# Softmax and values by halves in three attention units of a two-layer decode step

## The chip, the core and the metric

The kernel runs on one core of a Trainium2 chip. The core has five engines with an instruction stream each: TensorE (PE in the profile; its weight loads are shown apart as PEld), VectorE (DVE), ScalarE (ACT), GpSimd (POOL) and SyncE (SP), which here only issues transfers. Work on different engines is ordered by semaphores alone. The metric is the device time of one execution in microseconds (us); lower is better.

## The reference

Two equal layers are applied to four tokens (batch B = 4, model width 512), each a cached attention and then a gated unit, both behind a layer norm:

```python
q = (layernorm(x) @ wq)                       # 32 heads of 128
k = repeat(k_cache, 4); v = repeat(v_cache, 4)  # 8 heads of 4096 x 128 in the cache
p = softmax(q @ k.T * 128 ** -0.5)
x = x + (p @ v) @ wo
g, u = layernorm(x) @ w_gate, layernorm(x) @ w_up   # width 1792
x = x + (sigmoid(g) * u) @ w_down
# ... and the same again with the same weights and caches
```

All inputs are bf16. The caches are 33.6 MB each for K and for V, and both layers read them.

## The kernel before, in words

**Units.** The attention is cut into 16 units. A unit is one token `b`, one half `hg` of the cache heads (four of eight) and one layer `l`. Their order is written out in the list `seq`. Units 5, 9, 13 and 15 are (0,0,1), (1,0,1), (2,0,1) and (3,0,1): the last unit of a token, in layer two, with heads 0 to 3. Units 6, 10 and 14 are the units (b,1,1) of the next token.

**Tiles and the ring.** K and V come in tiles of 128 x 2048 bf16 (512 KB): one cache head, and one half `q` of the positions. So a unit has eight K tiles (q = 0: four heads, q = 1: four heads) and eight V tiles. They share a ring of 23 slots in the on-chip memory. The K tiles and seven of the V tiles of a unit (b,1,0) are kept in their slots until unit (b,1,1) has used them, so that layer two loads just one tile for that unit. While they are kept, eight slots are left for all the others. That is so when units 5, 9 and 13 stream their sixteen tiles, and right after each of them a unit with kept tiles follows.

**A unit before.** `unit_scores` transposes each K tile in place on VectorE (L656, a 32 x 32 block transpose) and then, for each q, issues 16 score matmuls into half of the bank pair `S_ps` (L663) as one block. `unit_probs` takes one maximum over all 1024 columns (L677) and spreads it over the heads by a transpose, a minimum and a transpose (L678, L680, L686). ScalarE writes the exponentials with their sums (L689). Eight matmuls into `PT_ps` (L696), a copy (L701), sixteen matmuls (L707) and a copy (L715) turn them into `pt_sb`. A sum over partitions (L721) and a reciprocal (L725) give the weight `wcol`. `unit_values` multiplies by V: 16 matmuls for q = 0 and 16 for q = 1, both accumulated in `O_ps` (L739). It scales the result into `o_sb` (L745), transposes it (L750), copies it to `oT` (L760) and multiplies by `wo` in 64 small matmuls (L766); L781 adds it to the token's state. When both head halves of a token are done, `chain` runs the gated unit (`layer_norm` L793 to L808, `rstd` L817 to L826, `glu` L842 to L894) and, after layer one, the queries of layer two (`second_q`, L614 and L620; `spread`, L634 and L641, which writes the score operand `qbd`).

**What sets the order.** Nothing is ordered by hand. Every step is put into a plan (`_Plan.put`) with an engine, a cost in us, a rank (the unit's number; half a unit more for its chain) and what it reads and writes. `schedule` then runs a list schedule when the kernel is built: each engine takes the step that can start first, the lower rank first among equals, and may wait a little for a lower rank (`PATIENCE`). The order of the transfers on SP's queue is fixed: in unit i, V of unit i - 1 and then K of unit i. A transfer into the ring waits for all users of the tile that held its slot; which slot that is, the plan decides by its own times. PE's time in the plan (`_Tensor`) has two speeds, as the clock gate has, and a wait at each block of instructions that has to be fetched (`PAGE`, `FETCH`). Where the plan sees PE idle, it puts in filler matmuls into an unused bank (`F_ps`, L936), which keep the clock up. `emit` writes each engine's stream in the planned order, with waits on semaphores, so a plan that is wrong in its times is still carried out in its order.

**Locks.** The PSUM bank `M_ps` is shared by many short steps. A step with `lock="M"` takes it and one with `free="M"` gives it back. `G_ps` and `U_ps` are used by the gated unit and by `second_q`.

## Time and profile before

| | |
|---|---|
| median of three runs | 332.08 us (331.55 to 333.64) |
| profiled execution, its own time | 331.62 us |
| span of its instructions | 329.7 us |
| mean granted TensorE clock | 0.948 |
| DVE busy | 177.5 us (54%) |
| ACT busy | 64.6 us (20%) |
| PE busy, fillers included | 291.7 us (88%); L936, the fillers, 137.3 us of it |
| DMA | 117.34 MB, mean 356 GB/s |

A line of the profile gives an engine, a kernel line, an operation, what it writes and reads, and its shape (partitions x elements). In the groups, "busy" is the time of all of them, then follow the mean duration in ns and the idle time of the engine before them. In a timeline, the first number is the start and the second the duration of a merged run, both in us, and the end of the line in brackets is the idle time before it and what ended it. "SPq" is SP's queue, which issues transfers; a transfer's issue is not its landing. In a table of stretches each row has a stretch's bounds, its length, the busy time and the number of instructions of each engine, the granted clock, the busy share of the DMA engines and their rate.

### The profile page before, as it was taken

Reading aid. Unit: us, or ns where it says so; the run is one execution under the profiler, and the core shown is the slowest. Engines: PE = TensorE matmul, PEld = TensorE weight load, DVE = VectorE, ACT = ScalarE, POOL = GpSimd, SP = SyncE. Lnnn points to the kernel's source line nnn. Section 1 sums busy time; section 2 is a strip of 40 time slices with the busy share of each in tenths; the row PEclk is TensorE's granted clock in tenths of the full one; section 3 lists DMA queues with packets and bytes.
Section 4 is the critical chain, followed back from the end, with each engine's and each line's share of the span. In section 5 each row is a group of like instructions: output and inputs, shape, how many; then the busy total and the mean of one; then the engine's idle time right before and its main releaser. Section 6 shows DMA issues by size and latency. Waiting matters only on the chain.

```text
span 329.7 us, 10495 instructions
## 1 busy us (share of the span) xinstructions
PE 291.7 (88%) x4772; PEld 143.2 (43%) x4772; DVE 177.5 (54%) x325; ACT 64.6 (20%) x137; POOL 12.3 (4%) x36
## 2 busy tenths in 40 slices
PE   6998999989979878989888689998869999998986
PEld 2534434434454433453454244543444444644433
DVE  5771482009613863942874828735827649329602
ACT  1202102002021312121223032121332121313221
POOL 5100000000000000000000000000000000000000
PEclk9997999999997999987997999969997999879999
DMA  7999999999999999698999999888999998979910
GB/s 278 380 410 408 410 371 356 408 411 406 381 357 366 416 408 408 238 352 285 393 412 409 408 407 397 291 325 329 416 407 410 407 409 268 361 263 412 408 59 0
DMA packets 35408, 117.34 MB, mean 356 GB/s; under 512 B 3364, under 2 KB 7716, under 8 KB 35364
## 3 DMA queue, kind: packets, MB, share of 16 engines
q1 hardware_dynamic: 35312, 116.67, 92.9%
q8 instruction: 37, 0.61, 0.7%
q14 instruction: 7, 0.06, 0.0%
q10 hardware_dynamic: 52, 0.01, 0.0%
HBM read 116.66 MB, written 0.00 MB: 354 GB/s over the span
## 4 chain that ended last, share of the span: by engine, by line
DMA 33%; PE 27%; SPq 17%; issue 13%; DVE 6%; ACT 3%; POOL 1%; ACTq 0%; POOLq 0%; DVEq 0%
DMA ring<-in_A_k_cache_dram 19%; SPq L486 13%; DMA wo<-in_A_wo_dram 6%; PE S_ps L663 5%; PE F_ps L936 5%; PE O_ps L739 4%; DMA wd_r<-in_B_w_down_dram 4%; SPq L489 4%; DMA ring<-in_A_v_cache_dram 4%; DVE ring L656 3%; PE U_ps L614 3%; PE U_ps L886 2%; ACT p_sb L689 1%; PE M_ps L766 1%; PE G_ps L842 1%
## 5 line engine op out<-in xcount | busy, mean ns | idle before, releaser
L656 DVE STREAM_TRANSPOSE ring<-ring 128x1024 int32<-128x1024 int32 x96 | 116.4, 1232 | 51.2 <-DMA ring<-in_A_k_cache_dram 50.4
L936 PE MATMUL F_ps<-ident 128*128 128x512 bf16 x524 | 137.3, 392 | 3.3 <-POOL stat L437 3.3
L936 PEld LDWEIGHTS F_ps<-ident 128*128 128x128 bf16 x524 | 47.8, 102 | 62.4 <-issue 17.4
L663 PE MATMUL S_ps<-ring,qbd 128*16 128x512 bf16 x512 | 39.8, 433 | 4.9 <-DVE ring L656 4.7
L739 PE MATMUL O_ps<-ring,pt_sb 128*16 128x512 bf16 x512 | 36.8, 418 | 7.0 <-DMA ring<-in_A_v_cache_dram 4.0
L677 DVE TENSOR_REDUCE ml<-S_ps 128x1 f32<-128x1024 f32 x16 | 19.6, 1224 | 34.0 <-PE S_ps L663 34.0
L689 ACT ACTIVATE p_sb<-S_ps,tr 128x1024 bf16<-128x1024 f32 x16 | 17.8, 1113 | 54.7 <-DVE tr L686 53.9
L745 ACT ACTIVATE o_sb<-O_ps,stat 128x512 bf16<-128x512 f32 x16 | 11.0, 687 | 77.8 <-PE O_ps L739 77.8
L739 PEld LDWEIGHTS O_ps<-ring,pt_sb 128*16 128x16 bf16 x512 | 12.4, 94 | 28.7 <-issue 15.2
L663 PEld LDWEIGHTS S_ps<-ring,qbd 128*16 128x16 bf16 x512 | 12.1, 94 | 23.8 <-DVE ring L656 9.8
L766 PE MATMUL M_ps<-wo,oT 128*1 128x128 bf16 x1024 | 17.2, 219 | 2.5 <-issue 1.7
L614 PE MATMUL U_ps<-xT,wq 128*128 128x1 bf16 x512 | 15.6, 164 | 3.9 <-issue 3.7
L826 POOL TENSOR_TENSOR stat<-stat 128x1 f32<-128x1 f32 x12 | 6.5, 540 | 302.9 <-DVE stat L822 264.4
L614 PEld LDWEIGHTS U_ps<-xT,wq 128*128 128x128 bf16 x512 | 14.8, 97 | 6.6 <-issue 5.1
L766 PEld LDWEIGHTS M_ps<-wo,oT 128*1 128x1 bf16 x1024 | 14.2, 83 | 6.8 <-ACT oT L760 3.8
L725 DVE RECIPROCAL stat<-M_ps 128x1 f32<-128x1 f32 x16 | 2.7, 166 | 20.9 <-PE M_ps L721 20.9
L859 ACT ACTIVATE p_sb<-G_ps,stat 128x256 f32<-128x256 f32 x8 | 3.8, 475 | 46.1 <-POOL stat L826 33.4
L701 ACT ACTIVATE p_sb<-PT_ps 128x512 bf16<-128x512 f32 x16 | 9.5, 597 | 12.3 <-PE PT_ps L696 12.3
L715 ACT ACTIVATE pt_sb<-PT_ps 128x512 bf16<-128x512 f32 x16 | 9.6, 598 | 11.7 <-PE PT_ps L707 11.7
L842 PE MATMUL G_ps<-wg,xT 128*1 128x448 bf16 x128 | 9.0, 351 | 2.6 <-DVE xT L799 2.1
L707 PE MATMUL PT_ps<-p_sb,ident 128*32 128x128 bf16 x256 | 7.7, 244 | 3.3 <-ACT p_sb L701 1.9
L641 DVE TENSOR_TENSOR qbd<-M_ps,stat 128x256 bf16<-128x256 f32 x16 | 6.5, 404 | 7.6 <-PE M_ps L634 7.6
(92 smaller groups left out, 177.5 us busy)
## 6 DMA issues: line engine op xcount, KB each, us to landing
ring<-in_A_v_cache_dram SPq DMA_DIRECT2D x100, 512.0 KB, 13.8
ring<-in_A_k_cache_dram SPq DMA_DIRECT2D x96, 512.0 KB, 12.8
wq<-in_A_wq_dram SPq DMA_DIRECT2D x2, 2048.0 KB, 14.3
wo<-in_A_wo_dram SPq DMA_DIRECT2D x4, 1024.0 KB, 14.7
wg<-in_B_w_gate_dram SPq DMA_DIRECT2D x1, 1792.0 KB, 13.5
wu<-in_B_w_up_dram SPq DMA_DIRECT2D x1, 1792.0 KB, 18.2
wd<-in_B_w_down_dram SPq DMA_DIRECT2D x1, 1536.0 KB, 22.6
wd_r<-in_B_w_down_dram SPq DMA_DIRECT2D x2, 128.0 KB, 18.4
```

Of the source, the lines that this page charges most:

```text
L486: S.put("sp", lambda e: e.dma_start(ring[t.slot], src), dma="ring", load=t, size=0.524, cost=0.45)
L489: S.put("sp", lambda e: e.dma_start(o, i), writes=[key], dma=key, size=size * pace, cost=0.45)
L614: fns.append(lambda e, g=g, k=k, c0=c0, c=c: e.matmul(U_ps[:, 16 + c:17 + c], lhsT=wq[:, g // NS, k, c0:c0 + DH], rhs=xT[:, b, k:k + 1], s ...
L656: "dve", lambda e, t=t: e.transpose(ring[t.slot].bitcast(dt.int32), ring[t.slot].bitcast(dt.int32)),
L663: fns.append(lambda e, s=s, t=t, nn=nn, q=q: e.matmul(S_ps[32 * s:32 * s + 16, q * 512:(q + 1) * 512], lhsT=qbd[:, qi, nn, s, :], rhs=ring ...
L677: dve(lambda e: e.tensor_reduce(ml[:, 0:1], S_ps[:], AX.X, ALU.max, negate=True), ["S0", "S1"], ["ml"], 1.22)
L689: lambda e: e.activation(p_sb[:].rearrange("p c x -> p (c x)"), S_ps[:], ACTF.Exp, bias=tr[:, 0:1], accum_out=ls),
L739: fns.append(lambda e, s=s, v=v, c=c, cc=cc: e.matmul(O_ps[32 * s:32 * s + 16, :], lhsT=pt[:, c, s, :, :].rearrange("p t h -> p (t h)"), r ...
L745: "act", lambda e: e.activation(o_sb[:], O_ps[:], ACTF.Copy, scale=wcol[:, i % 2:i % 2 + 1]),
L766: fns.append(lambda e, n=n, j=j: e.matmul(M_ps[32 * j:32 * j + 1, P:2 * P], lhsT=oT[:, i % 2, n:n + 1], rhs=wo[:, hg * 16 + n, j * P:(j + ...
L842: fns.append(lambda e, k=k, j=j: e.matmul(o_ps[32 * j:32 * j + 1, 0:FS], lhsT=xT[:, b, k:k + 1], rhs=w[:, k, j * FS:(j + 1) * FS], start=( ...
L936: lambda e: e.matmul(F_ps[:], lhsT=ident[:], rhs=ident[:].unsqueeze(1).broadcast_to([P, 4, P]), start=True, stop=True,),
```

## The change

In units 5, 9 and 13 the softmax and the product with V are done separately for q = 0 and q = 1. Each half has its own maximum, exponentials, sums and transposed weights (`half_probs`), right behind its scores. Each half of V goes into its own bank, q = 0 into `O_ps` and q = 1 into `G_ps` (`half_values`). `half_weights` works out two weights from the two maxima and sums, by which the two results are scaled when they are copied to `o_sb`; their transposes are added up in columns 32 to 47 of `U_ps`. In the same units the scores are issued for two K tiles at a time (eight matmuls) and not for four.

The plan changes as well. A fetched block of instructions counts 126.2 matmuls instead of 128, the count starts at 25.5, and the fp32 matmuls, which are two instructions in the trace, count twice (`wide`). Every step that gives back the bank M gets rank -1, so it goes ahead of all others that could start at the same time.

The diff, cut to its core:

```diff
@@ -18,7 +18,8 @@
 WINDOW = 3.413
 BUSY_UP = 0.8
 BUSY_DOWN = 0.6
-PAGE = 128
+PAGE = 126.2
+PAGE_AT = 25.5
 FETCH = 5.8
 PE_GAP = 0.1
 FILL_FROM = 0.0
@@ -34,7 +35,7 @@
         self.fast = False
         self.window = 0.0
         self.busy = 0.0
-        self.count = 0
+        self.count = PAGE_AT
         self.page = {0: 0.0, 1: 0.0}
 
...
         todo = n
-        while todo:
-            p, at = divmod(self.count, PAGE)
+        while todo > 1e-3:
+            p = int((self.count + 1e-3) / PAGE)
             t = max(t, self.page[p])
             if p + 1 not in self.page:
                 self.page[p + 1] = t + FETCH
-            k = min(PAGE - at, todo)
+            k = min(PAGE * (p + 1) - self.count, todo)
             t = self._part(t, quick * k / n, slow * k / n)
             self.count += k
             todo -= k
...
+        self.words = len(fns)
...
-    def put(self, eng, fns, reads=(), writes=(), cost=0.1, rank=0.0, dma=None, size=0, lock=None, free=None, tiles=(), load=None, cold=None):
+    def put(self, eng, fns, reads=(), writes=(), cost=0.1, rank=0.0, dma=None, size=0, lock=None, free=None, tiles=(), load=None, cold=None, wide=False):
         if not isinstance(fns, (list, tuple)):
             fns = [fns]
         op = _Op(len(self.ops), eng, list(fns), cost, rank, dma or eng, 16 if dma else 1)
         op.size, op.lock, op.free, op.tile = size, lock, free, load
+        op.words *= 2 if wide else 1
+        if free is not None:
+            op.rank = -1.0
...
-            clock[e] = tensor.run(at, op.cost, op.cold, len(op.fns)) if e == "pe" else at + op.cost
+            clock[e] = tensor.run(at, op.cost, op.cold, op.words) if e == "pe" else at + op.cost
...
+    ls2 = stat[:, 41:43]
+    nbh = stat[:, 43:45]
+    nbm = stat[:, 45:46]
+    e2 = stat[:, 46:48]
+    j2 = stat[:, 48:50]
+    wh = stat[:, 56:58]
+    lt = stat[:, 58:59]
+    HALF = (5, 9, 13)
...
-    def unit_scores(i):
+    def half_scores(i, q, parts):
         b, hg, l = seq[i]
         qi, rank = i % 2, float(i)
-        for q in range(2):
-            ts = [tile("k", b, hg, l, s, q) for s in range(NS)]
-            for s, t in enumerate(ts):
+        for part in parts:
+            ts = [(s, tile("k", b, hg, l, s, q)) for s in part]
+            for s, t in ts:
                 if fresh("k", hg, l, s, q):
                     S.put(
                         "dve", lambda e, t=t: e.transpose(ring[t.slot].bitcast(dt.int32), ring[t.slot].bitcast(dt.int32)),
@@ -659,17 +672,149 @@
                     t.users.append(S.ops[-1])
             fns = []
             for nn in range(NQ):
-                for s, t in enumerate(ts):
+                for s, t in ts:
                     fns.append(lambda e, s=s, t=t, nn=nn, q=q: e.matmul(
                         S_ps[32 * s:32 * s + 16, q * 512:(q + 1) * 512],
                         lhsT=qbd[:, qi, nn, s, :],
                         rhs=ring[t.slot].rearrange("p (t bb j r) -> p t bb j r", bb=2, j=32, r=2)[:, :, nn // 2, :, nn % 2],
                         start=(nn == 0), stop=(nn == NQ - 1),
                     ))
-            S.put("pe", fns, reads=[f"qbd{qi}"], writes=[f"S{q}"], tiles=ts, cost=0.86, rank=rank)
+            S.put("pe", fns, reads=[f"qbd{qi}"], writes=[f"S{q}"], tiles=[t for s, t in ts], cost=0.86, rank=rank)
+
+    def half_probs(i, q):
+        rank = float(i)
+        s_ps = S_ps[:, q * 512:(q + 1) * 512]
+        pk = ("p_sb", "p_hi")[q]
+
+        def dve(fn, reads, writes, cost):
+            S.put("dve", fn, reads=reads, writes=writes, cost=cost, rank=rank)
+
+        dve(lambda e: e.tensor_reduce(ml[:, 0:1], s_ps, AX.X, ALU.max, negate=True), [f"S{q}"], ["ml"], 0.68)
+        dve(lambda e: e.transpose(tr[:], ml[:]), ["ml"], ["tr"], 0.22)
+        dve(
+            lambda e: e.tensor_reduce(
+                ml[:].rearrange("p (x h) -> p x h", h=R),
+                tr[:, 0:16].rearrange("p (a h) -> p h a", h=R).unsqueeze(1).broadcast_to([P, 8, R, 4]), AX.X, ALU.min,
+            ),
+            ["tr"], ["ml"], 0.4,
+        )
+        dve(lambda e: e.transpose(tr[:], ml[:]), ["ml"], ["tr"], 0.22)
+        S.put(
+            "act",
+            lambda e: e.activation(
+                p_sb[:, 4 * q:4 * q + 4, :].rearrange("p c x -> p (c x)"), s_ps, ACTF.Exp, bias=tr[:, 0:1],
+                accum_out=ls2[:, q:q + 1],
+            ),
+            reads=[f"S{q}", "tr"], writes=[pk, f"ls2{q}"], cost=0.82, rank=rank,
+        )
+        S.put(
+            "act", lambda e: e.activation(nbh[:, q:q + 1], tr[:, 0:1], ACTF.Copy),
+            reads=["tr"], writes=[f"nbh{q}"], cost=0.2, rank=rank,
+        )
...
+        S.put("pe", fns, reads=[pk, "ident"], writes=["PT"], cost=0.11, rank=rank)
+        S.put(
+            "act",
+            lambda e: e.activation(
+                p_sb[:, 4 * q:4 * q + 2, :].rearrange("p u x -> p (u x)"), PT_ps[:, q * 256:(q + 1) * 256], ACTF.Copy
+            ),
+            reads=["PT"], writes=[pk], cost=0.4, rank=rank,
+        )
...
+        S.put("pe", fns, reads=[pk, "ident"], writes=["PT"], cost=0.16, rank=rank)
+        pt = pt_sb[i % 2]
+        S.put(
+            "act",
+            lambda e: e.activation(
+                pt[:, 4 * q:4 * q + 4].rearrange("p c s t h -> p t (c s) h"),
+                PT_ps[:, q * 256:(q + 1) * 256].rearrange("p (t x h) -> p t x h", t=4, h=R), ACTF.Copy,
+            ),
+            reads=["PT"], writes=[f"pt_sb{i % 2}" + ("", "x")[q]], cost=0.4, rank=rank,
+        )
+
+    def half_weights(i):
+        rank = float(i)
+        S.put(
+            "pe", lambda e: e.matmul(M_ps[:, 20:22], lhsT=hsum[:], rhs=ls2, start=True, stop=True),
+            reads=["ls20", "ls21", "hsum"], writes=[bank("M", True)], cost=0.2, rank=rank, lock="M",
+        )
+        S.put(
+            "dve", lambda e: e.tensor_tensor(nbm, nbh[:, 0:1], nbh[:, 1:2], ALU.min),
+            reads=["nbh0", "nbh1"], writes=["nbm"], cost=0.16, rank=rank,
+        )
+        S.put(
+            "act", lambda e: e.activation(e2, nbh, ACTF.Exp, bias=nbm, scale=-1.0),
+            reads=["nbh0", "nbh1", "nbm"], writes=["e2"], cost=0.22, rank=rank,
+        )
+        S.put(
+            "dve",
+            lambda e: e.scalar_tensor_tensor(
+                out=j2, in0=M_ps[:, 20:22], scalar=1.0, in1=e2, op0=ALU.mult, op1=ALU.mult, accum_out=lt
+            ),
+            reads=[bank("M"), "e2"], writes=["lt", "j2"], cost=0.24, rank=rank, free="M",
+        )
+        S.put("dve", lambda e: e.reciprocal(lt, lt), reads=["lt"], writes=["lt"], cost=0.17, rank=rank)
+        S.put(
+            "dve", lambda e: e.tensor_scalar(wh, e2, lt, None, op0=ALU.mult),
+            reads=["e2", "lt"], writes=["wh"], cost=0.17, rank=rank,
+        )
+
+    def half_values(i, q, parts):
+        b, hg, l = seq[i]
+        rank = float(i)
+        pt = pt_sb[i % 2]
+        o_ps = (O_ps, G_ps)[q]
+        for part in parts:
+            ts = [(s, tile("v", b, hg, l, s, q)) for s in part]
+            fns = []
...
+            S.put(
+                "pe", fns, reads=[f"pt_sb{i % 2}" + ("", "x")[q]], writes=[("O", "G")[q]],
+                tiles=[t for s, t in ts], cost=0.86, rank=rank,
+            )
+        S.put(
+            "act", lambda e: e.activation(o_sb[:], o_ps[:], ACTF.Copy, scale=wh[:, q:q + 1]),
+            reads=[("O", "G")[q], "wh"], writes=["o_sb"], cost=0.7, rank=rank,
+        )
+        S.put(
+            "pe", [
+                lambda e, t4=t4: e.matmul(
+                    U_ps[:, 32:48], lhsT=o_sb[:, t4 * P:(t4 + 1) * P], rhs=id_b[:, :, 4 * t4:4 * t4 + R],
+                    start=(q == 0 and t4 == 0), stop=(q == 1 and t4 == 3),
+                ) for t4 in range(4)
+            ],
+            reads=["o_sb", "ident"], writes=["U"], cost=0.11, cold=0.11, rank=rank,
+        )
+
+    def unit_scores(i):
+        parts = [(0, 1), (2, 3)] if i in HALF else [(0, 1, 2, 3)]
+        for q in range(2):
+            half_scores(i, q, parts)
+            if i in HALF:
+                half_probs(i, q)
 
     def unit_probs(i):
...
+        if i in HALF:
+            half_weights(i)
+            return
...
-            reads=["ls", "hsum"], writes=[bank("M", True)], cost=0.2, rank=rank, lock="M",
+            reads=["ls", "hsum"], writes=[bank("M", True)], cost=0.2, rank=rank, lock="M", wide=True,
...
-    def unit_values(i):
+    def whole_values(i):
...
+    def unit_values(i):
+        b, hg, l = seq[i]
+        rank = float(i)
+        if i in HALF:
+            for q in range(2):
+                half_values(i, q, [(0, 1, 2, 3)])
+        else:
+            whole_values(i)
         o = oT[:, i % 2, :]
         S.put(
             "act",
-            lambda e: e.activation(o, M_ps[:, 0:16], ACTF.Copy),
-            reads=[bank("M")], writes=[f"oT{i % 2}"], cost=0.22, rank=rank, free="M",
+            lambda e: e.activation(o, U_ps[:, 32:48] if i in HALF else M_ps[:, 0:16], ACTF.Copy),
+            reads=["U" if i in HALF else bank("M")], writes=[f"oT{i % 2}"], cost=0.22, rank=rank,
+            free=None if i in HALF else "M",
         )
...
-            reads=[f"xsum{b}", f"x{b}", f"xs{c}", "ones", "sel4"], writes=["U"], cost=0.36, cold=0.8, rank=rank,
+            reads=[f"xsum{b}", f"x{b}", f"xs{c}", "ones", "sel4"], writes=["U"], cost=0.36, cold=0.8, rank=rank, wide=True,
...
-            reads=[f"xsqc{b}", "onesA"], writes=[bank("M", True)], cost=0.2, rank=rank, lock="M",
+            reads=[f"xsqc{b}", "onesA"], writes=[bank("M", True)], cost=0.2, rank=rank, lock="M", wide=True,
...
```

22 lines of the change are left out of this document (21 added, 1 removed).

## The prediction, made before the changed kernel was run

> **What bounds the kernel now.** I read the stretches first: busy time and DMA rate by stretch of time.
>
> ```profile
> 113.00:134.00 21.00, 16.93 (x296) 7.54 (x288) 13.20 (x20) 4.14 (x8) 0.00 (x0) 1.00 1.03 410
> 134.00:146.00 12.00, 10.79 (x228) 6.27 (x228) 8.68 (x22) 2.17 (x5) 0.73 (x2) 0.97 0.76 256
> 146.00:160.00 14.00, 12.92 (x209) 5.96 (x206) 5.37 (x11) 2.23 (x5) 0.35 (x1) 0.78 0.93 329
> 160.00:205.00 45.00, 38.51 (x713) 18.98 (x717) 29.74 (x49) 10.83 (x22) 1.00 (x2) 0.96 1.03 407
> 205.00:217.00 12.00, 11.33 (x226) 6.51 (x218) 8.41 (x20) 2.89 (x7) 0.62 (x2) 0.86 0.89 303
> 217.00:231.00 14.00, 12.02 (x213) 5.53 (x205) 6.88 (x17) 1.62 (x4) 0.22 (x1) 0.88 0.88 328
> 274.00:286.00 12.00, 11.45 (x268) 7.41 (x264) 8.29 (x20) 3.13 (x8) 1.08 (x2) 0.97 0.86 281
> 286.00:298.00 12.00, 10.95 (x192) 4.74 (x192) 3.54 (x8) 1.65 (x4) 0.00 (x0) 0.75 0.82 308
> ```
>
> The last column is GB/s. Outside three stretches the stream of K and V runs at 405 to 410, and no engine can make it faster; I call 409 full. Inside them it starves: 12 x (1 - 256/409) = 4.5 us and 14 x (1 - 329/409) = 2.7 in the first, 3.1 and 2.8 in the second, 3.8 and 3.0 in the third. That is 11.4 in the three front parts, 8.5 in the rear parts, 19.9 in all. They lie at units 5, 9 and 13, where only eight slots are free.
>
> Next come the waits of SP's queue and the timelines of the first stretch, to see what is late:
>
> ```profile
> SPq L311 <- PE S_ps L663: 56.5, 11, 10.1
> SPq L486 <- PE O_ps L739: 23.6, 8, 6.1
> ...
> 126.66 0.33 SPq L486 DMA_DIRECT2D ring<-in_A_k_cache_dram  x1
> 137.13 13.60 SPq L486 DMA_DIRECT2D ring<-in_A_v_cache_dram  x9
> 150.77 4.88 SPq L486 DMA_DIRECT2D ring<-in_A_k_cache_dram  x8
> ...
> 130.00 2.53 DVE L656 STREAM_TRANSPOSE ring<-ring 128x1024 int32<-128x1024 int32 x2
> 135.96 1.08 PE L663 MATMUL S_ps<-ring,qbd 128*16 128x512 bf16 x16
> 148.47 1.88 PE L663 MATMUL S_ps<-ring,qbd 128*16 128x512 bf16 x16
> 150.14 1.92 PE L739 MATMUL O_ps<-ring,pt_sb 128*16 128x512 bf16 x16
> ```
>
> **Front part.** The last K tile is issued at 126.66; then SP waits for the scores of q = 0 (135.96 to 137.04) and issues the first V tile at 137.13. The landing events of the trace put that K tile at 137.5 and that V tile at 141.5: a queue that has run dry needs 4.4 us from issue to landing, and a tile takes 1.27 in a full stream. But the second K tile of the unit was transposed by 131.3. Only the block of four tiles, and the gated unit's matmuls ahead of it on PE, kept two slots until 137. **Rear part.** The first four V tiles have landed by 146.7, and the next slot is free at 150.4, after scores of the kept unit 6 at 148.47; values of unit 5 come at 150.14, because `pt_sb` needs the maximum over both halves (L677 at 140.98, the last copy of L715 at 148.65). In the third stretch the same values run at 287.26 and the next issue is at 289.19. The second is like these.
>
> **The change, part by part.**
>
> *Pairs.* The same matmuls, 2 x 8 for 16; the first pair can run at 131.3 + 8 x 0.07 (1.08 us for 16). V's first two issues move from 137.1 to about 132, before the queue is dry; 137.5 - 4.4 = 133.1 was needed. Front gain: 4.5, 3.1, 3.8, less what the last pair of q = 1 leaves. By the rows that pair needs the last transpose (139.7), the half's extra DVE work (next) and its own 0.6, so 142.4; its V tiles, seventh and eighth behind K at 1.27 each, land at 146.4 without a hole and should be issued at 142.0. I leave 0.5 per stretch; at worst PE is again held by L842 and L886 (1 to 2 us), which is all of the gain.
>
> *Half maxima.* Per unit a second L678, L680, L686 (0.21 + 0.37 + 0.21) and two reductions over 512 columns for one over 1024 (1.224). No row has that shape; each lies between 0.61 (half) and 1.22 (all of it). I take 0.66, near the half: L865 falls from 0.42 to 0.35 between 256 and 192 columns, almost in step with them. `half_weights` adds three steps like L725 and L808 (0.17 each). DVE: 0.79 + 0.10 + 0.5 = 1.4 us per unit, at most 2.5. The first half's four steps with their gaps, some 1.9, fall between the q = 1 transposes, and there DVE has no room: from 128.7 to 139.7 it works almost without a break and ends 0.9 behind the last landing. So the last transpose ends some 2 us later, which is counted above.
>
> *Half exponentials and copies on ACT.* L689 (1.11 + 0.19) becomes twice 0.65 to 1.3; L701 and L715 (0.60) twice 0.35 to 0.6 (L859 with 256 columns: 0.475); L745 (0.69) doubles. Some 2 to 3 us more per unit; ACT is busy 2.2 of the 14 us at 146 to 160 and 3.1 of the 12 at 274 to 286, so this costs nothing unless a half step stands ahead of the gated unit's tanh (a rival below).
>
> *Half values.* q = 0's chain runs while q = 1's K tiles land; its V tiles land by 142.6, values run 142.7 to 143.8, and four slots are free at 143.9, not 150.4. V of q = 1 lands until 147.7, so the next tile, issued at 143.9 + 4.4 = 148.3, costs 0.6. Further slots are due at 149 (values of q = 1, or unit 6's scores at 148.5). Rear gain 2.7, 2.8, 3.0, less 0.7 each. Worst: zero, if these slots wait for the kept unit all the same.
>
> *What is late next.* After the first stretch SP again waits for slots: the last V tile of unit 7 is issued at 167.94, after a hole of 7 us in SP's timeline, and lands 9.0 us later, 4.6 more than a dry queue needs. With the stream 6 us ahead, and unit 6 only some 4 to 5 ahead (its exponential waits for `p_hi`, behind unit 5's gated unit), I give back 0.8, and 0.8 after the second.
>
> After the third the end is not the stream's:
>
> ```profile
> 297.02 1.25 DVE L656 STREAM_TRANSPOSE ring<-ring 128x1024 int32<-128x1024 int32 x1 [1.01 <-DMA ring<-in_A_k_cache_dram]
> 305.25 3.48 DVE L656 STREAM_TRANSPOSE ring<-ring 128x1024 int32<-128x1024 int32 x3
> 310.07 1.22 DVE L677 TENSOR_REDUCE ml<-S_ps 128x1 f32<-128x1024 f32 x1 [1.35 <-PE S_ps L663]
> 317.58 1.04 PE L739 MATMUL O_ps<-ring,pt_sb 128*16 128x512 bf16 x16 [0.62 <-DMA ring<-in_A_v_cache_dram]
> ```
>
> Unit 15 stays whole. DVE works without a break from 297.0 to 308.7 (eight transposes, 10 us, and 1.7 of others), and the way from there to `pt_sb` takes until 315.87; the last V tile lands at 317.54. If K comes 5.5 us earlier, unit 14's maximum (2.3 us, now 293.7 to 296.0, just ahead) and later steps of unit 13 (0.9) fall into this run: 291.5 + 11.7 + 3.2 = 306.4, only 2.3 to 2.7 earlier. `pt_sb` at 313.2, then 32 matmuls in 2.1: values end at 315.3 and not at 318.62. So the third stretch gives 3.3, not its 6.8 - 1.2.
>
> *Plan constants.* `PAGE`, `wide` and rank -1 add no instruction; they shuffle the order. The trace shows what blocks cost: pieces of 1.2 to 2.3 us of "issue" inside PE groups in the chain. Planning them better gains up to 2 us, a worse order loses as much (patience for rank -1 idles DVE at most a third of a transpose). I take 0.4 lost. The Trainium skill's page Runtime: NRT & Kernel Launch (section Instruction fetch mechanics) holds that crossing a block is mostly hidden; by it this term is 0, and these pieces speak against it.
>
> **Sum.** 7.2 - 1.2 - 0.8 = 5.2; 5.9 - 1.2 - 0.8 = 3.9; 3.3; less 0.4: 12.0. From the span, 329.7 - 12.0 = 317.7; the profiled execution has 1.9 outside the span, 319.6, and the median of the runs lies 0.5 above it: **320 us**.
>
> **Rivals.**
> 1. *Only the pairs work.* V slots of q = 0 come no earlier than unit 6's scores; the half chains land in PE's and ACT's queues too late. For it: before, the rear slots came from scores of the kept unit in two of three stretches. Against: 287.26 in the third. Front 11.4 - 1.5, third stretch capped at 3.3, 0.4 lost: 4.0 + 2.6 + 3.3 - 0.4 = 9.5, near 323.
> 2. *All of it and nothing given back.* Each stretch loses 1 us and the end follows the stream: 19.9 - 3 = 17 to 18, near 314. Against: DVE's run at the end.
> 3. *The order undoes it: no change.* The plan's pair costs 0.86 as the four did (a measured pair is about half), so PE's plan is off by up to 1.7 us per unit; a pair placed behind L842, L886 or L614 frees nothing early. Holes move, 328 to 335.
> 4. *Slower: the other token's chain pays.* ACT and DVE run in order. If the first half's maximum (1.9 us) and ACT steps (1.8) stand ahead of the chain of unit 4, 8 or 12 (L799 to L894, then L614), `qbd` of the kept unit comes 3.7 us later, and so do its eight slots: scores at 152, not 148.5. With the rear gain lost and 3.7 x 3 = 11 more starvation against a front gain halved to 5.7: 5.4 slower, near 337. It decides from the point where the kept unit's first scores start over 12 us after the last K landing (now 10.9, 9.1, 11.7). Against: chain ranks (4.5, 8.5, 12.5) go before the half's (5, 9, 13) whenever both can start.
>
> **How the numbers follow.** Forecast 0.45, rival 1 0.22, rival 2 0.12, rival 3 0.10, rival 4 0.11. A measurement of this kernel tells about 1% (3.3 us) from no change. Faster by more: the first three and a little of rival 3, 0.80; within: 0.09; slower by more: 0.11. Range: below, rival 2 with the plan's 2 us and a little, 311; above, rival 3 nearly whole, 334. That leaves out rival 4 and the edges, about 0.15.
>
> **What would show it.** Right: at 134 to 160 and its two fellows 380 GB/s or more; V's first issue of units 5, 9, 13 at least 4 us before the last K landing; L739's q = 0 block right behind the fourth V landing; DVE without a break in the last K tiles, and `pt_sb` of unit 15 after its last V landing. Wrong: a first pair behind L842 on PE; the kept unit's scores later than now; stream rates below 400 between the stretches.

## The result, and the profile after

The changed kernel takes **327.54 us** (median of four runs, 326.84 to 337.07) against 331.99 before: a ratio of 0.987, 95% interval 0.982 to 0.992. An execution over 1.5% slower than the fastest of its kernel, like the one at 337.07, counts in the medians below but not in the ratios, and where such a one was profiled a table has a dash. The forecast was 320. The direction came, and 4.5 of the 12 us.

The profiled execution took 326.88 us, with a span of 324.9 and a granted clock of 0.937. First its stretches of time: bounds, length, busy time of PE, PEld, DVE, ACT and POOL, granted clock, DMA share, GB/s.

```profile
134.00:146.00 12.00, 11.60 (x230) 6.49 (x230) 9.97 (x26) 2.50 (x8) 0.54 (x1) 0.86 0.99 351
146.00:160.00 14.00, 12.75 (x291) 6.68 (x283) 7.01 (x25) 3.53 (x10) 0.54 (x1) 0.88 1.01 363
...
205.00:217.00 12.00, 9.96 (x224) 5.75 (x222) 6.95 (x23) 4.49 (x14) 0.54 (x1) 1.00 0.95 321
217.00:231.00 14.00, 12.82 (x212) 5.69 (x213) 7.42 (x19) 2.93 (x7) 0.54 (x1) 0.88 1.02 387
274.00:286.00 12.00, 10.79 (x270) 7.29 (x270) 6.31 (x16) 2.59 (x11) 0.54 (x1) 0.78 0.79 269
286.00:298.00 12.00, 11.76 (x203) 5.31 (x202) 7.82 (x21) 3.28 (x8) 0.54 (x1) 0.80 1.00 368
```

The stream still starves at units 5, 9 and 13, though less; these windows are fixed in time while the work in them comes up to 8 us earlier than before. So I also counted the holes from the landing events: each landing's distance from the one before, less the size of the tile at full rate, summed over the three stretches. "Next" are the nine tiles that follow V of unit 5, 9 or 13.

| us lost in the stream | V, q = 0 | V, q = 1 | next | all |
|---|---|---|---|---|
| before | 10.0 | 2.3 | 8.6 | 20.9 |
| after | 0.7 | 7.4 | 5.0 | 13.1 |

The hole ahead of V is closed. Another has opened four tiles later, at V of q = 1, and the rear hole is a good half of what it was. From the last landing of V of units 4, 8 and 12 to the next such mark or the end, the stages were 70.2, 69.1 and 60.9 us and are now 66.2, 67.7 and 60.3. The first mark itself moved from 127.4 to 128.6. So the gains are 4.0, 1.4 and 0.6, less 1.2. These are figures of one execution each: the changed kernel profiled once more (after_again below) lost 1.7, 6.1 and 7.2 us, with stages of 67.3, 68.6 and 60.3, so a single one holds to some 2 us.

The timeline of the first stretch, after (start, duration, line, operation; in brackets the idle time before it and what ended it):

```profile
132.53 1.03 PE L676 MATMUL S_ps<-ring,qbd 128*16 128x512 bf16 x8 [2.31 <-DVE ring L669]
133.65 13.03 SPq L499 DMA_DIRECT2D ring<-in_A_v_cache_dram  x9
139.59 0.93 PE L997 MATMUL U_ps<-wu,xT 128*1 128x448 bf16 x16
140.35 1.03 PE L676 MATMUL S_ps<-ring,qbd 128*16 128x512 bf16 x8
143.72 1.07 PE L676 MATMUL S_ps<-ring,qbd 128*16 128x512 bf16 x8 [0.17 <-DVE ring L669]
144.88 1.79 SPq L499 DMA_DIRECT2D ring<-in_A_v_cache_dram  x3
145.26 1.04 PE L784 MATMUL O_ps<-ring,pt_sb 128*16 128x512 bf16 x16
150.72 1.73 PE L784 MATMUL G_ps<-ring,pt_sb 128*16 128x512 bf16 x16 [1.12 <-DMA ring<-in_A_v_cache_dram]
152.58 1.88 PE L676 MATMUL S_ps<-ring,qbd 128*16 128x512 bf16 x16
```

V's first issue comes at 133.65, 5.2 us ahead of the last K landing (138.85). But the first pair of q = 1, transposed by 137.65, runs at 140.35, behind the gated unit's L997. The last pair waits for the last transpose, which ends 4.8 us after the last landing (2.2 before); the third V tile of q = 1 is issued only at 144.88. That is 6.0 us after the last K landing, where the forecast had 4.9 (142.4 after 137.5) and 4.5 was needed. Then the kept unit 6 finds its scores at 152.58 behind the values of q = 1, which wait for V. Its first scores start 13.7, 14.2 and 14.1 us after the last K landing of units 5, 9 and 13 (before: 10.9, 9.0, 11.7).

In the third stretch both pairs are late, and for the first of them it is DVE that is late:

```profile
269.25 1.24 DVE L669 STREAM_TRANSPOSE ring<-ring 128x1024 int32<-128x1024 int32 x1
271.10 0.69 DVE L692 TENSOR_REDUCE ml<-S_ps 128x1 f32<-128x512 f32 x1
273.89 2.36 DVE L669 STREAM_TRANSPOSE ring<-ring 128x1024 int32<-128x1024 int32 x2
275.64 1.03 PE L676 MATMUL S_ps<-ring,qbd 128*16 128x512 bf16 x8
276.42 1.24 DVE L669 STREAM_TRANSPOSE ring<-ring 128x1024 int32<-128x1024 int32 x1
277.07 3.71 SPq L499 DMA_DIRECT2D ring<-in_A_v_cache_dram  x5
278.27 1.04 PE L784 MATMUL O_ps<-ring,pt_sb 128*16 128x512 bf16 x16 [1.06 <-DMA ring<-in_A_v_cache_dram]
279.24 0.55 PE L627 MATMUL U_ps<-xT,wq 128*128 128x1 bf16 x16
279.88 1.37 PE L627 MATMUL U_ps<-xT,wq 128*128 128x1 bf16 x48
281.18 1.88 PE L676 MATMUL S_ps<-ring,qbd 128*16 128x512 bf16 x8
```

The fifth K tile is transposed by 270.49 and the sixth only from 273.89 on: between them DVE does the first half's maximum (L692 and what follows it) and steps of the gated unit. So the first pair of q = 1 runs at 275.64, and the first V tile of q = 1 is issued at 277.07, 4.3 us after the last K landing (272.7). That is 2.2 of the 3.6 us that V of q = 1 loses here. The last pair's tiles are ready at 277.66 (end of the last L669 row). It starts at 281.18, behind the values of q = 0 (L784), which wait for their fourth V tile, and behind the layer-two queries of the gated unit (L627), and it runs slowly (1.88). Its slots come free for tiles behind V; the last two V tiles go into slots of the values of q = 0.

The end, which answers to the rows of unit 15 before:

```profile
298.14 2.36 DVE L669 STREAM_TRANSPOSE ring<-ring 128x1024 int32<-128x1024 int32 x2
301.32 3.48 DVE L669 STREAM_TRANSPOSE ring<-ring 128x1024 int32<-128x1024 int32 x3
306.14 1.23 DVE L822 TENSOR_REDUCE ml<-S_ps 128x1 f32<-128x1024 f32 x1 [1.35 <-PE S_ps L676]
312.00 1.90 PE L884 MATMUL O_ps<-ring,pt_sb 128*16 128x512 bf16 x32
```

The last V tile lands at 310.2 and no longer matters: the values wait for `pt_sb` (L860). Unit 15's transposes end at 304.8, 4.8 us after its last K landing (2.8 before), for DVE does unit 14's maximum and the gated unit of unit 13 among them.

Last, the groups of the score matmuls, from the pages of before and of after (busy time, mean ns of one, idle before). The number of matmuls is the same.

```profile
L663 PE MATMUL S_ps<-ring,qbd 128*16 128x512 bf16 x512 | 39.8, 433 | 4.9 <-DVE ring L656 4.7
```

```profile
L676 PE MATMUL S_ps<-ring,qbd 128*16 128x512 bf16 x512 | 47.3, 439 | 6.0 <-DVE ring L669 5.9
```

7.5 us more for the same 512 matmuls. A pair of eight takes 1.03 to 1.11 us in ten of twelve cases (median 1.07), and a block of sixteen 1.11 (median of 26): both as long. By these medians, twelve pairs in place of six blocks make some 6.2 of the 7.5.

### The profile page after: what moved, and what is told of

Its sections match the earlier page's. It is cut to its first block, busy times and chain, and to the rows that moved or that the text cites. A ratio compares the mean times of both kernels' runs of the same rounds, so it can differ in the third digit from the quotient of the medians.

```text
span 324.9 us, 10574 instructions
## 1 busy us (share of the span) xinstructions
PE 288.7 (89%) x4784; PEld 141.9 (44%) x4784; DVE 182.2 (56%) x349; ACT 69.7 (21%) x161; POOL 12.3 (4%) x36
## 5 line engine op out<-in xcount | busy, mean ns | idle before, releaser
L669 DVE STREAM_TRANSPOSE ring<-ring 128x1024 int32<-128x1024 int32 x96 | 115.7, 1228 | 45.4 <-DMA ring<-in_A_k_cache_dram 44.7
L1091 PE MATMUL F_ps<-ident 128*128 128x512 bf16 x476 | 124.6, 393 | 3.3 <-POOL stat L450 3.3
L1091 PEld LDWEIGHTS F_ps<-ident 128*128 128x128 bf16 x476 | 44.5, 103 | 57.2 <-issue 15.7
L676 PE MATMUL S_ps<-ring,qbd 128*16 128x512 bf16 x512 | 47.3, 439 | 6.0 <-DVE ring L669 5.9
L884 PE MATMUL O_ps<-ring,pt_sb 128*16 128x512 bf16 x416 | 28.8, 414 | 2.7 <-DMA ring<-in_A_v_cache_dram 1.3
L822 DVE TENSOR_REDUCE ml<-S_ps 128x1 f32<-128x1024 f32 x13 | 15.9, 1222 | 23.8 <-PE S_ps L676 23.8
L834 ACT ACTIVATE p_sb<-S_ps,tr 128x1024 bf16<-128x1024 f32 x13 | 14.5, 1113 | 57.3 <-DVE tr L831 52.7
L890 ACT ACTIVATE o_sb<-O_ps,stat 128x512 bf16<-128x512 f32 x13 | 8.9, 687 | 59.1 <-PE O_ps L884 57.1
L884 PEld LDWEIGHTS O_ps<-ring,pt_sb 128*16 128x16 bf16 x416 | 10.3, 94 | 19.6 <-issue 8.4
L627 PE MATMUL U_ps<-xT,wq 128*128 128x1 bf16 x512 | 15.6, 164 | 1.8 <-issue 1.8
L627 PEld LDWEIGHTS U_ps<-xT,wq 128*128 128x128 bf16 x512 | 14.6, 99 | 5.8 <-issue 3.7
L1014 ACT ACTIVATE p_sb<-G_ps,stat 128x256 f32<-128x256 f32 x8 | 3.8, 474 | 45.2 <-POOL stat L981 45.2
L936 DVE SCALAR_TENSOR_TENSOR xs<-M_ps,xs 128x128 f32<-128x128 f32 x12 | 3.3, 278 | 11.5 <-PE M_ps L921 11.4
L860 ACT ACTIVATE pt_sb<-PT_ps 128x512 bf16<-128x512 f32 x13 | 7.8, 597 | 8.7 <-PE PT_ps L852 8.7
L997 PE MATMUL G_ps<-wg,xT 128*1 128x448 bf16 x128 | 8.8, 351 | 0.2
```

The source lines that it names most:

```text
L627: fns.append(lambda e, g=g, k=k, c0=c0, c=c: e.matmul(U_ps[:, 16 + c:17 + c], lhsT=wq[:, g // NS, k, c0:c0 + DH], rhs=xT[:, b, k:k + 1], s ...
L669: "dve", lambda e, t=t: e.transpose(ring[t.slot].bitcast(dt.int32), ring[t.slot].bitcast(dt.int32)),
L676: fns.append(lambda e, s=s, t=t, nn=nn, q=q: e.matmul(S_ps[32 * s:32 * s + 16, q * 512:(q + 1) * 512], lhsT=qbd[:, qi, nn, s, :], rhs=ring ...
L822: dve(lambda e: e.tensor_reduce(ml[:, 0:1], S_ps[:], AX.X, ALU.max, negate=True), ["S0", "S1"], ["ml"], 1.22)
L834: lambda e: e.activation(p_sb[:].rearrange("p c x -> p (c x)"), S_ps[:], ACTF.Exp, bias=tr[:, 0:1], accum_out=ls),
L860: lambda e: e.activation(pt[:].rearrange("p c s t h -> p t (c s) h"), PT_ps[:].rearrange("p (t x h) -> p t x h", t=4, h=R), ACTF.Copy),
```

## The experiments

The expectations name the theories by letters: A, time on PE's queue; B, the operations that the halves add, on DVE above all; C, the plan's constants; D, eight slots for the stream, so that a hole closed at one place opens at the next; E, the end hangs on the other token's chain; F, the holes of the stream set the time; G, the order on PE. Each edit is made to the changed kernel, but for one. Holes are in us over the three stretches, from one profiled execution each.

| kernel | median us | ratio to before (95%) | V q=0 | V q=1 | next |
|---|---|---|---|---|---|
| constants_only | 334.28 | 1.008 (1.003 to 1.013) | 7.5 | 7.6 | 7.8 |
| old_constants | 330.51 | 0.994 (0.991 to 0.998) | 3.1 | 10.8 | 5.4 |
| pairs_only | 333.80 | 1.006 (1.003 to 1.010) | 0.3 | 3.2 | 19.1 |
| halves_only | 339.28 | 1.020 (1.014 to 1.025) | 7.8 | 16.5 | 2.3 |
| no_max | 333.35 | 1.004 (1.000 to 1.008) | 0.6 | 4.8 | 8.3 |
| pe_first | 334.58 | 1.000 (0.994 to 1.007) | 0.0 | 10.3 | 3.7 |
| late_max | 334.14 | 1.005 (1.000 to 1.009) | – | – | – |
| no_max_pe_first | 331.33 | 0.999 (0.994 to 1.004) | 0.0 | 2.3 | 6.8 |
| half_5_9 | 333.31 | 1.004 (1.001 to 1.007) | – | – | – |
| half15 | 328.62 | 0.992 (0.987 to 0.996) | 1.5 | 8.1 | 5.6 |
| cut_after | 324.15 | 0.980 (0.974 to 0.985) | 2.9 | 6.2 | 2.4 |
| cut_before | 329.10 | 0.993 (0.989 to 0.996) | 10.8 | 3.4 | 7.4 |
| pert_fetch | 330.91 | 0.997 (0.993 to 1.002) | 0.4 | 14.0 | 3.2 |
| pert_lat | 327.98 | 0.990 (0.986 to 0.994) | – | – | – |
| after_again | 327.83 | 0.987 (0.981 to 0.993) | 1.7 | 6.1 | 7.2 |
| sc_first | 329.93 | 0.995 (0.991 to 1.000) | 0.0 | 9.3 | 3.7 |
| pairs_q0 | 335.88 | 1.012 (1.008 to 1.017) | 1.1 | 19.2 | 2.7 |
| tanh_after | 330.23 | 0.994 (0.990 to 0.999) | 0.1 | 9.1 | 4.7 |

**The parts alone.** The plan's constants without halves or pairs:

```diff
-    HALF = (5, 9, 13)
+    HALF = ()
```

> The plan's new constants (blocks of 126.2 matmuls, fp32 counted twice, rank -1 for the steps that give back M) with no unit in halves. Theory A (what is left of the holes comes from PE's queue: pairs and half values stand behind the other token's chain): the constants only reorder, 330 to 334 us, the three stretches starve as before (18 to 22 us in all). Theory B (DVE: the half maxima delay the last transposes): the same, 330 to 334. Theory C (the plan's constants made the difference): 327 to 328.5 if they bring the gain, 335 or more if they cost it.

Halves and pairs with the constants of before:

```diff
-PAGE = 126.2
-PAGE_AT = 25.5
+PAGE = 128
+PAGE_AT = 0
-        op.words *= 2 if wide else 1
+        pass
-            op.rank = -1.0
+            pass
```

> Halves and pairs as in the change, with the plan's old constants and no rank -1. Theory A: 326 to 330, like the change. Theory B: the same. Theory C: 331 to 333 if the constants bring the gain; 318 to 323, what was forecast, if they cost it.

Pairs without halves:

```diff
-            if i in HALF:
-                half_probs(i, q)
...
-        if i in HALF:
-            for q in range(2):
-                half_values(i, q, [(0, 1, 2, 3)])
-        else:
-            whole_values(i)
+        whole_values(i)
```

> Scores in pairs of K tiles in units 5, 9 and 13 and the new constants, but one softmax and one accumulation of the values as before. Theory A: the front parts of the stretches starve 4 to 6 us less than before in all, the rear parts as before (8.5): 326 to 329. Theory B: DVE has no half maxima, so the front parts close nearly whole (9 to 11 us): 321 to 324.

Halves without pairs:

```diff
-        parts = [(0, 1), (2, 3)] if i in HALF else [(0, 1, 2, 3)]
+        parts = [(0, 1, 2, 3)]
```

> Softmax and values by halves in units 5, 9 and 13 and the new constants, but the scores in one block of four tiles. Theory A: the front parts starve as before (11.4 us), the rear parts 2 to 4 us less: 328 to 331. Theory B: the maxima delay the transposes and nothing makes up for it: 332 to 336.

Neither part alone gains anything. Both kernels have the new constants, which cost 0.8% by themselves; against constants_only pairs alone are level (0.998) and halves alone 1.2% slower, and the two together 2.1% faster. With pairs alone the front hole is closed (0.3) and all of it turns up behind V, where no slot comes free before the values of both halves:

```profile
134.43 20.99 SPq L499 DMA_DIRECT2D ring<-in_A_v_cache_dram  x9
153.16 3.13 PE L879 MATMUL O_ps<-ring,pt_sb 128*16 128x512 bf16 x32
155.46 4.80 SPq L499 DMA_DIRECT2D ring<-in_A_k_cache_dram  x8
```

SP's queue takes 21 us over nine V tiles, and the next K tile is issued at 155.46, after the values (146.72 in the changed kernel). With halves alone the rear is mended (2.3) and V starves (24.3 in both halves of q). So D holds for a part alone: the holes move and stay 22.6 and 26.6 us in all, and only both together bring the sum down to 13.1. The constants alone cost 0.8%, and with halves and pairs they gain 0.7%: they add no instruction but a few fillers, so what they change is the order, and its worth depends on the rest. They may also change what comes ahead of the first stretch: V of unit 4 has landed at 127.4 before and in old_constants, at 128.6 in constants_only and in the changed kernel, and at 128.7 to 130.1 in three other executions with the changed kernel's sequence up to there.

**Operations or order.** The half maxima taken out (the exponentials have bias 0, and the weights no factor from the maxima):

```diff
-        dve(lambda e: e.tensor_reduce(ml[:, 0:1], s_ps, AX.X, ALU.max, negate=True), [f"S{q}"], ["ml"], 0.68)
-        dve(lambda e: e.transpose(tr[:], ml[:]), ["ml"], ["tr"], 0.22)
...
```

> The change without the half maxima: in units 5, 9 and 13 the exponentials are taken with no maximum taken off, so eight steps on DVE, the copies of the maxima and the exponential of their difference are left out. Theory A (PE's queue): the V tiles of q = 1 still come late, holes there 5 to 7 us of 7.4; 325 to 329 us. Theory B (DVE's half maxima between the transposes): holes before the q = 1 V tiles fall to 1 to 3 us; 321 to 324. Theory D (eight slots: a hole that is closed at one place opens at the next as long as the values do not run earlier): the q = 1 hole falls but the hole before the next unit's tiles grows by most of it; 325 to 328.

The scores and values of units 5, 9 and 13 at rank -1, ahead of the other token's chain on PE:

```diff
-            S.put("pe", fns, reads=[f"qbd{qi}"], writes=[f"S{q}"], tiles=[t for s, t in ts], cost=0.86, rank=rank)
+            S.put("pe", fns, reads=[f"qbd{qi}"], writes=[f"S{q}"], tiles=[t for s, t in ts], cost=0.86, rank=-1.0 if i in HALF else rank)
...
-                tiles=[t for s, t in ts], cost=0.86, rank=rank,
+                tiles=[t for s, t in ts], cost=0.86, rank=-1.0,
```

> The change with rank -1 for the score blocks and value blocks of units 5, 9 and 13, so that PE takes them ahead of the other token's chain. Theory A: the last pairs and the values start within 0.5 us of their operands, q = 1 holes 3 to 4 us of 7.4 and holes before the next unit's tiles 2 to 3 of 5.0; 321 to 324 us. Theory B: PE was not what they waited for; all holes within 1.5 us of 13.1, 326 to 328.5. Theory D: between the two.

The first half's maximum after the transposes of q = 1 (the second line makes a write of `ml` wait for its readers):

```diff
-            S.put("dve", fn, reads=reads, writes=writes, cost=cost, rank=rank)
+            S.put("dve", fn, reads=reads, writes=writes, cost=cost, rank=rank + (0.2 if q == 0 else 0.0))
-                self._after(op, r, True)
+                self._after(op, r, k != "ml")
```

> The change with the first half's four maximum steps ranked behind the transposes of the q = 1 tiles on DVE (and with a wait for the earlier reader of that tile). Theory B: transposes no longer wait for maxima, q = 1 holes fall from 7.4 to 1 to 3 us; if that is all, 321 to 324. Theory D: they fall so, but the values of q = 0 come later and the holes before the next unit's tiles grow from 5.0 to 10 or more; 329 to 333. Theory A: q = 1 holes stay at 5 or more.

The edits of no_max and pe_first together:

> Both: no half maxima (left out as in the kernel without them) and score and value blocks of units 5, 9 and 13 first on PE. Theories A and B together: holes in the three stretches 3 to 6 us in all, the stream ends near 303 to 305 and the end is set by unit 15's own softmax; 317 to 321 us. Theory D alone: holes of 8 or more remain, 323 or more.

None of the four gained on the changed kernel; no_max lost 1.7% although it does less. At V of q = 1 it did what theory B says, though by less: the last transposes end 1.6, 1.6 and 2.1 us after the last K landing and not 4.8, 3.9 and 4.9, and V of q = 1 loses 4.8 us and not 7.4. But more is lost behind it (8.3), and the last stage takes 62.4 us. So the half maxima do delay V of q = 1, and taking them out does not bring the missing time, as far as a kernel whose order changes along can say. In pe_first the kept unit's first scores start 17.4, 10.8 and 18.0 us after the last K landing: taking this unit's PE work ahead of the other token's chain makes the kept slots late. In no_max_pe_first the holes are the smallest of all (9.1), and the time is that of before: the tail behind the stream's last landing is 16.0 us, against 12.6 in the changed kernel. Holes alone (F) don't set the time either.

**Which units.** Without unit 13, and with unit 15:

```diff
-    HALF = (5, 9, 13)
+    HALF = (5, 9)
```

> The change without the third unit: halves and pairs in units 5 and 9 alone. Theory E (the end hangs on a chain through the tokens: values of unit 12, gated unit, queries, scores of the kept unit 14, its maximum ahead of unit 15's transposes on DVE; from the last V landing of unit 12 to the end 60 us whatever the stream does): 326 to 329 us, that stretch 59 to 62. Theory F (holes of the stream set the time): the 7 us of holes of the third stretch come back, 331 to 334.

```diff
-                self._after(op, r, True)
+                self._after(op, r, k != "ml")
-    HALF = (5, 9, 13)
+    HALF = (5, 9, 13, 15)
```

> The change with unit 15 in halves and pairs as well (and a wait for the earlier reader of the maxima's tile). Theory E: from unit 15's last transpose to the end it takes 18.0 us; a half maximum, half exponential and half copies save 2 to 3: 324 to 326 us. Theory F: the last V tile sets the end, 327 to 329.

With two units the gain is gone (1.004), much more than the third stage showed (0.6). Up to the scores of unit 13 (266.4 us in the changed kernel) PE, DVE and ACT carry out the same sequence in both kernels, fillers aside, so the loss lies behind them: under the same plan the halves of unit 13 are worth 1.7%, although against the kernel before its stage gained little. What a whole unit 13 waits for under this plan stays open. With halves in unit 15 the last stage is 58.9 us and not 60.3, and the time does not fall. The marks ahead of it came later in the profiled execution (129.1, 197.7 and 266.1 against 128.6, 194.8 and 262.5), although the three engines carry out the same sequence up to there: this is the spread between executions, and 1.4 us cannot be told from it.

**The other token's chain.** The kept units 6, 10 and 14 take their queries from layer one, so that they need not wait for the gated unit (their result is then another); once in the changed kernel and once in the kernel before:

```diff
-        if l == 0:
+        if l == 0 or hg == 1:
```

> The change with the queries of layer one in the kept units 6, 10 and 14, so that their scores do not wait for the other token's gated unit; its work is all done, but the result of these units is another. Theory E: the kept units' first scores start 10 us or less after the last K landing (14 in the change), 55 to 58 us from unit 12's last V landing to the end, 318 to 323 us in all. Theory G (PE's order holds them: second-half values stand ahead and wait for late V tiles): 325 to 328.

> The kernel before with the same: queries of layer one in the kept units 6, 10 and 14. Theory E: kept scores 2 to 5 us earlier than 9 to 12 us after the last K landing, 324 to 329 us. Theory F: the holes at V of q = 0 stay (10 us) and the time with them, 330 to 333. Theory G: as E, since there is no half value block ahead of them.

This takes the wait for the gated unit away. The kept units' first scores start 5.5, 2.9 and 2.2 us after the last K landing in cut_after; in cut_before they start at 7.6, 9.0 and 10.5, not much earlier than before (10.9, 9.0 and 11.7). Taking the wait away gains 0.7% before and, by the quotient 0.980 / 0.987, 0.7% after, each with some half a percent of doubt. The change is worth 1.3% with and without that wait. So the wait is worth some 2 us in both kernels, and it is not shown to be what the change lacks. The last stage stays at 61.7 and 61.2 us.

**The same operations in another order.** Two of the plan's constants, moved a little, and the kernel itself once more:

```diff
-FETCH = 5.8
+FETCH = 5.6
```

> The changed kernel with one constant of the order's plan moved a little (FETCH from 5.8 to 5.6); the operations are the changed kernel's, one for one, and only the order differs: both pairs of scores of q=1 stand behind all four blocks of the gated unit's queries on PE, as in the kernel with the old constants (330.51). Theory G, the order decides: 329.5 to 331.5, and the values' second transfers lose 10 us or more over the three stretches, as they did there (10.8). Theory B, the operations decide and the order is a detail: 327 to 328.5, with a loss near the changed kernel's 7.4.

```diff
-LATENCY = 0.05
+LATENCY = 0.06
```

> The changed kernel with another constant of the plan moved a little (LATENCY from 0.05 to 0.06); the same operations, and here the first pair of q=1 stays ahead of the gated unit's tail, as in the changed kernel. Theory G, the order decides: 326 to 328.5, with 7.4 us or less lost at the values' second transfers. If it lands at 330 or more with the pairs in the same place, the place of the pair is not what sets the difference between the kernels of the same operations.

> The changed kernel itself once more, to stand beside the three others on the same chip. All theories: 326.8 to 328.2, a ratio near 0.987.

pert_fetch lost what was expected, and at the place that was expected: 14.0 us at V of q = 1. DVE and PE in the second stretch of it, and then in the changed kernel:

```profile
206.98 0.69 DVE L692 TENSOR_REDUCE ml<-S_ps 128x1 f32<-128x512 f32 x1
209.11 1.24 DVE L669 STREAM_TRANSPOSE ring<-ring 128x1024 int32<-128x1024 int32 x1
210.76 0.55 PE L627 MATMUL U_ps<-xT,wq 128*128 128x1 bf16 x16
211.39 1.34 PE L627 MATMUL U_ps<-xT,wq 128*128 128x1 bf16 x48
212.66 1.98 PE L676 MATMUL S_ps<-ring,qbd 128*16 128x512 bf16 x14
```

```profile
202.87 1.23 DVE L669 STREAM_TRANSPOSE ring<-ring 128x1024 int32<-128x1024 int32 x1
204.82 0.68 DVE L692 TENSOR_REDUCE ml<-S_ps 128x1 f32<-128x512 f32 x1
209.00 1.08 PE L676 MATMUL S_ps<-ring,qbd 128*16 128x512 bf16 x8
210.24 1.74 PE L627 MATMUL U_ps<-xT,wq 128*128 128x1 bf16 x64
```

In pert_fetch both pairs of q = 1 stand behind the four query blocks, as was expected; V's first tile of q = 1 is issued at 214.5, 6.8 us after the last K landing (207.8). But the queries are the smaller part of this. DVE does the maximum of q = 0 (L692) ahead of the sixth K tile, which is transposed by 210.35, 2.6 us after the last landing; PE then adds 2.3 us. In the changed kernel the sixth tile goes ahead of the maximum and is done at 204.10, 1.0 us before the last landing; the first pair runs right behind it, and that V tile is issued at 205.4, 0.4 after the landing of 205.1. From 203 to 231 the stream runs at 294 GB/s in pert_fetch and at 360 in the changed kernel.

The scores alone at rank -1 (the first edit of pe_first without the second):

> The changed kernel with the pairs of scores alone at rank -1, so that PE's plan takes them ahead of the other token's chain; the values keep their rank, unlike in the kernel with both ahead (334.58). In all three stretches the first pair of q = 1 stands ahead of the gated unit's queries then. Theory G, the order decides, by the place of this pair: 325 to 328. If it lands at 330 or more, the place of the first pair alone is not the thing in the order that decides, and what waits behind the pairs counts as well.

It lands between both of its expectations, at 0.995, with 9.3 us lost at V of q = 1; its profiled execution was its fastest run (326.02), so the trace doesn't stand for the median. The place of the first pair in PE's order is not all.

Read together, the traces point to DVE: V of q = 1 starves where the maximum of q = 0 is done ahead of the sixth of the unit's eight transposes. Each cell has the three stretches, of units 5, 9 and 13:

| kernel | transposes ahead of that maximum | end of the sixth, us after the last K landing | us lost at V, q = 1 |
|---|---|---|---|
| the changed kernel | 6, 6, 5 | -1.2, -1.0, 2.4 | 1.7, 2.1, 3.6 |
| pert_fetch | 6, 5, 5 | -0.8, 2.6, 2.1 | 1.4, 7.2, 5.4 |
| pe_first | 5, 5, 5 | 1.3, 1.9, 2.4 | 2.3, 3.6, 4.4 |
| sc_first | 5, 5, 5 | 0.4, 1.9, 2.3 | 1.7, 3.8, 3.8 |
| no_max_pe_first | no maximum | -1.3, -0.4, 0.2 | 0.0, 0.5, 1.8 |

Where PE takes the pairs first, this maximum can start earlier, and DVE takes it ahead of the sixth tile. This fits that pe_first and sc_first did not close the hole, and that with the maxima left out the same rank on PE leaves only 2.3 us of it. It is read from the traces and not shown by an edit of its own: in late_max, which moves the maximum, the order on PE changes too.

The five orders of the same operations (fillers aside, 460 to 482 of them) give 0.987, 0.990, 0.995, 0.997 and 1.000: order alone is worth as much as the whole change, and the ends are apart (the changed kernel's interval ends at 0.992, that of pe_first begins at 0.994).

**The pair's cost, and the end.** Pairs for q = 0 alone:

```diff
-        parts = [(0, 1), (2, 3)] if i in HALF else [(0, 1, 2, 3)]
         for q in range(2):
+            parts = [(0, 1), (2, 3)] if i in HALF and q == 0 else [(0, 1, 2, 3)]
```

> The changed kernel with pairs for q = 0 alone; the scores of q = 1 are one block of four tiles again. In the changed kernel a pair of eight matmuls takes 1.07 us, as long as the block of sixteen (1.10), so the pairs cost PE about 1 us per half that the forecast left out. If PE's time is what the pairs pay with, one block for q = 1 gives it back: 325 to 327, with the loss at the values' second transfers at or under the changed kernel's 7.4. If the pair of q = 1 frees two slots that the queue needs, that loss grows, to 10 or more over the three stretches, and the time goes to 329 to 332.

PE saves a microsecond per unit and the kernel loses 8 us. The slots that the pairs of q = 1 free are worth far more than the PE time that they cost. In the first stretch of this kernel:

```profile
144.45 1.11 PE L676 MATMUL S_ps<-ring,qbd 128*16 128x512 bf16 x16 [0.18 <-DVE ring L669]
155.15 1.88 PE L784 MATMUL G_ps<-ring,pt_sb 128*16 128x512 bf16 x16 [2.52 <-DMA ring<-in_A_v_cache_dram]
```

All four slots of q = 1 come free at 145.6, and the values of q = 1 wait for V until 155.15 (150.72 in the changed kernel).

The gated unit's tanh in a buffer of its own (as bf16), so that the next kept unit's exponential need not wait for it:

```diff
-            (0, 2 * P, p_sb[:, 4:8, :].rearrange("p c x -> p (c x)").bitcast(dt.float32), "p_hi"),
-            (2 * P, FS, o_sb[:].bitcast(dt.float32)[:, 0:FS - 2 * P], "o_sb"),
+            (0, 2 * P, h_sb[:, 0:2 * P], h_key),
+            (2 * P, FS, h_sb[:, 2 * P:FS], h_key + "x"),
```

> The changed kernel with the gated unit's tanh written as bf16 where the values go later, so that the exponential of the next kept unit need not wait for the gated unit to be done with the shared buffer (in the changed kernel unit 14's exponential starts at 298.05, behind unit 13's gates). Theory E, the end hangs on the other token's chain: the last stage, from the landing of unit 12's values to the last operation, falls from 60.3 to 57 to 58.5, and the time to 324 to 326. Theory F, the holes of the stream set the time: the last stage stays within 1 us of 60.3 and the time follows the landings only, 326.5 to 328.5.

Unit 14's exponential starts at 294.4 instead of 298.05, and nothing follows: unit 15's transposes end at 305.5 (304.8), and the last stage is 61.0 us. This wait was not on the path, and E falls at this place. The last stage is 59 to 63 us in every kernel whose holes the table gives, and what holds it there is shown only in part: in the changed kernel as before, unit 15's transposes end 42 us after V of unit 12 has landed (42.3 and 42.1), and the end follows 18 to 19 us later. No run moves unit 14's maximum off DVE.

No kernel that computes the whole reference was faster than the changed one.

## Why the prediction was wrong

**The step that failed** is the residue in the front part, "I leave 0.5 per stretch" for the last pair of q = 1. It measured 1.7, 2.1 and 3.6 us, 7.4 in all and not 1.5 (6.1 in the second profile). With the rear (5.0, forecast 2.1) and V of q = 0 (0.7) the holes keep 13.1 of 20.9 us, where the forecast left 3.6 of 19.9.

What the runs showed in its place: the sum let the half maximum delay the last pair, and gave the first pair of q = 1 no delay. The last pair came about as late as forecast or 1.1 us later: the third V tile of q = 1 was issued 6.0 and 5.1 us after the last K landing in the first two stretches (4.9 forecast), and in the second it took 6.4 us to land and not 4.4, for which the traces give no reason. The first pair was late too. In the first stretch PE held it behind L997, which the forecast named as its worst case ("at worst PE is again held by L842 and L886"). In the third DVE held it, with the maximum of q = 0 and the gated unit's steps ahead of the sixth transpose. no_max shows the share of the maxima (4.8 in place of 7.4), and pert_fetch, with the same operations, what their place in the order is worth (14.0).

Point by point:
- *Pairs at the front:* right. V's first issue came 5.2, 5.1 and 5.2 us ahead of the last K landing (forecast 4 or more), and V of q = 0 lost 0.7 us. pairs_only shows that this is the pairs' work.
- *"The same matmuls, 2 x 8 for 16 … 8 x 0.07":* wrong by half. A pair costs 1.07, not 0.6. Of the residue this is 0.5 us per pair at most, and pairs_q0 shows that the cost is worth paying.
- *Half maxima:* right in size, and wrong in where they stand on DVE (the step above). 0.69 us for the maximum over 512 columns (0.66 taken), and the last transpose ended 2.6, 1.5 and 2.4 us later (some 2 forecast). The prediction's "ends 0.9 behind the last landing" is a misreading: 139.7 less 137.5 is 2.2. Its sum goes from 139.7, so nothing hangs on it.
- *ACT at nothing:* right. The half exponential takes 0.69, the copies 0.38, and no half step stands ahead of the tanh in the first stretch (L1014 at 140.19, the exponential at 140.87).
- *Half values:* half right. The values of q = 0 run 1.4, 1.3 and 0.1 us behind their fourth V landing, not at once, and the rear loses 5.0 instead of 8.6. Those of q = 1 wait for V, and in the first two stretches they hold up the kept unit's scores behind them; in the third those scores run ahead of them, at 286.77, behind query blocks and the second half's softmax. So the late scores came that rival 4 took as its sign, past its mark of 12 us in all three stretches. Its price did not come: the kernel got no slower, and cut_after and cut_before put the worth of the wait for the gated unit at the same 0.7% with the change and without.
- *Given back:* 0.8 for each of the first two stretches. In the second the holes shrank by 2.7 (6.4 to 3.7) and the stage by 1.4, so 1.3; in the first 3.7 and 4.0, so nothing.
- *The end:* the mechanism was right, and unit 15's softmax sets the end (values at 312.00 behind `pt_sb`, last V landing 310.2). The run of DVE over unit 15's K tiles took 15.5 us (14.9 forecast, 11.7 before). What was missing is the headway: the first of these transposes stood 26.8 us behind V of unit 12 (289.3 less 262.5), 30.4 before, so 3.6 us came and not 5.5. Of that the longer run took 3.8, and 0.8 was won behind it: 0.6, not 3.3. (By the prediction's own 306.4 its sum gives 2.9; 3.3 takes the larger of its two values.)
- *Plan constants:* 0.4 forecast. The first mark came 1.2 us later, as in constants_only and not in old_constants; this is no more than the spread of that mark in one order. The rest of their effect is order and went the other way: with halves and pairs they gain 0.7%.

The difference to the forecast, by stages: 1.2 + 2.5 + 2.7 us in the three stretches and 0.8 ahead of them, 7.2 of the 7.5 between the medians. The rates between the stretches held (407 and 404 GB/s), as the forecast needed; 380 in the stretches did not come (357 in the first). Rival 3, that the order undoes it, was closest to the cause, with a chance of 0.10; its reason, that a pair takes half of the 0.86 planned, was not so (1.07).

The Trainium skill (Runtime: NRT & Kernel Launch, Instruction fetch mechanics) holds that crossing a block of instructions is mostly hidden, and by it the term for the constants would have been 0 (0.4 was taken). No run here isolates a block crossing: that the pieces of "issue" are what blocks cost is not shown, and what constants_only measured, 0.8%, comes with a changed order.

## What to carry to other kernels

In a stream through few slots, follow each slot to the next one: closing the first hole moved the starvation four tiles on, and neither half of the remedy gained anything alone. When an order comes from a greedy plan, an edit's worth is not the sum of its operations; compare it with the same operations in two or three other orders (a constant of the plan moved a little) before a difference of 1% is put down to the edit. And count what stands ahead of every step of a refill, on each engine that it passes: here a maximum that moved ahead of one transpose on DVE cost more than the matmuls ahead of the pair on PE (3.6 against 2.3 us in pert_fetch).
